# Six slots in the tile of wd for staged weight slices, and squares of wd placed between the last splits of gate and up

## The chip, the cores and the metric

The kernel runs on one core of a Trainium2 chip. The metric is the device time of one execution in microseconds, the median of several runs. The engines are TensorE (PE in the profile; its weight loads PEld), VectorE (DVE), ScalarE (ACT), GpSimd (POOL) and SyncE (SP), which does nothing here but issue DMA transfers, one after another in the order of the program.

## The reference

One transformer block whose two layer norms are modulated by a condition c: multi-query attention with 32 heads of width 16 over 2048 positions, then a feed-forward part with a bilinear gate, F = 1792.

```python
mod = (_silu(c) @ w_mod).reshape(c.shape[0], 6, 1, -1)
sa, ca, ga, sb, cb, gb = (mod[:, 0], mod[:, 1], mod[:, 2], mod[:, 3], mod[:, 4], mod[:, 5])
h = _layernorm(x, axis=-1) * (1 + ca) + sa
x = x + ga * _A_ref(h, A_wq, A_wk, A_wv, A_wo)          # softmax(q k^T / 4) v @ wo, one k and v for all heads
h = _layernorm(x, axis=-1) * (1 + cb) + sb
x = x + gb * _B_ref(h, B_w_gate, B_w_up, B_w_down)      # ((h @ w_gate) * (h @ w_up)) @ w_down
```

Everything is float32. The kernel reaches that precision by splitting each operand of a large product into two float16 halves, a high one and the rest, and adding three products.

## The kernel before, in words

**The long loop.** Attention is worked off in 32 units (8 blocks of 256 positions by 4 groups of heads), a unit in 16 turns over the keys, a turn in two steps: step = 32 × unit + 2 × turn. In a turn PE makes four score tiles (`sc`, L651), of which ACT takes the exponential (`P<-sc`, L653); four more tiles for the running maximum of the next unit (`mx`, L596), which DVE reduces (L600); the products with v (`pv`, L662); and as many side products (`side`, L506: projections of q, later wo, gate, up and down) as fit between. The order of all this is written out by hand, and every engine works in that order.

**A unit's end.** When a unit's last pv is done, in the second turn of the next unit, `pv_out` copies the result (`ev`, ACT L668) and issues ten transfers in a row on SP: two of row sums (`rs`, L673) and eight of 16 rows each (`oc`, L679). `normalise` then loads the row sums (`rc`, L686), takes reciprocals on DVE (L689) and spreads them (`ri`, `rr`). `load_q` fetches the q of the next unit (`sst<-qd`, L561), and `max_rows` writes the finished maxima to the same tile (`sst<-mt`, L634); both are SP transfers that PE's next scores or maxima need.

**The late weights.** `late_weights` makes a list of items for wo, gate, up and down (wd) that need their scales first. `side_step` takes at most one item per step, when the gap of the one before it is over; an item with `nothing` in the middle leaves its function for the start of the next turn. The list has these parts:

- `norms`: each of 36 slices (4 of wo, 16 of gate, 16 of up) is staged by an SP transfer (`stage`, L923, tile `wsl`, three buffers under the tag "xl"); an item later POOL squares it and adds it to an accumulator (`square`, L930 and L932). The accumulators `ssqs` and, from before, the blocks `hfs` of the first layer norm are both views of one large tile, kwb, whose place later holds the halves of wd. `ssqs[0]` serves wo and then gate, `ssqs[1]` up. Three items after a matrix is through, `sums` adds the partitions up on PE (L942), four matmuls a sum, four sums a matrix.
- `gcols`, `tr`, `bc`, `scales`, `inverse`: scales from the sums.
- `pipelined` for wo, gate and up: each slice is staged again, and an item later POOL scales it and writes its two halves (`split`, L1058 or L1064, L1065, L1066).
- `row_norms` for wd: each of 14 slices is staged, and two items later ACT squares it with a sum along the row (L976).
- `last_column` to `last_inverse`: the scale of wd.
- at the second unit, `dlist` is appended: the splits of wd, 14 slices with gap 2.25.

**kwb's layout.** In units of one slot of 512 float32 per partition, `hfs` is slots 0 to 11; `ssqs[0]` begins at slot 4 and is 3.5 slots long, `ssqs[1]` begins at slot 8:

```python
hfs = kwb[:, 0:2 * NHF * BT].bitcast(F32).rearrange("p (n t) -> p n t", n=NHF)
ssqs = [kwb[:, 2 * n * BT:2 * n * BT + 2 * F].bitcast(F32) for n in (KC, 2 * KC)]
```

The program tracks which parts of a tile an instruction reads and writes, and adds waits where they overlap. A transfer also waits for the eighth transfer before it: there are eight lanes, DMAHW0 to DMAHW7, taken in turn.

Of the kernel before, what the change touches and what calls it, by code (L numbers as in the profile page):

```python
# [13 lines left out]
F32 = mybir.dt.float32  # L14
F16 = mybir.dt.float16
AF = mybir.ActivationFunctionType
# [3 lines left out]
S, D, H, DH, F = 2048, 512, 32, 16, 1792  # L20
KC = D // 128
# [8 lines left out]
LEAD = 30  # L30
WARM = (21, 3, 2, 3)
SQ_GAP = 2.75
ROW_GAP = 1.75
SUM_GAP = 6.0
SUM_LAG = 3
SPLIT_GAPS = (2.25, 2.25)
LATE_Q = 3
NORM_AT = (5, 12, 18)
NBANK = 8
# [21 lines left out]
def adaln_mqa_glu_kernel(ctx: ExitStack, tc: tile.TileContext, x_in, wq_in, wk_in, wv_in, wo_in,  # L61
                         wg_in, wu_in, wd_in, c_in, wm_in, out):
    nc = tc.nc
# [5 lines left out]
    work = ctx.enter_context(tc.tile_pool(name="work", bufs=2))  # L69
# [7 lines left out]
    def ps_hold(name="side", shape=(128, 512)):  # L77

        tag, bufs = pool.popleft()
        t = psum.tile(list(shape), F32, name=name, tag=tag, bufs=bufs)  # L80
        held[id(t)] = (t, tag, bufs)
        return t
# [60 lines left out]
    for i in range(3):  # L143
        t = consts.tile([128, 2, BT], F16, name=f"sst{i}")
# [77 lines left out]
    hfs = kwb[:, 0:2 * NHF * BT].bitcast(F32).rearrange("p (n t) -> p n t", n=NHF)  # L222
# [595 lines left out]
    W = {}  # L818
# [56 lines left out]
    def wslices():  # L875
        for k in range(KC):
            yield 3, (k, slice(0, D)), wo_in[k * 128:(k + 1) * 128, :], D
        for m, v in ((0, wgv), (1, wuv)):
            for k in range(KC):
                for c in range(F // GC):  # L880
                    yield m, (k, slice(c * GC, (c + 1) * GC)), v[:, k, c * GC:(c + 1) * GC], GC
        for f in range(FT):
            yield 2, (f, slice(0, D)), wdv[:, f, :], D

    def late_weights():
        st = {}

        def m0(k):
            def f():
                if k == 0:  # L890
                    st["p"] = ps_hold("misc")
                for j, (w, col) in enumerate(((wmB[0], 0), (wmB[0], 512), (wmA, 1024), (wmB[0], 1024))):
                    nc.tensor.matmul(st["p"][32 * j:32 * j + 32, :], silr[:, k, 0:32], w[:, k, col:col + 512],
                                     start=(k == 0), stop=(k == KC - 1))
            return f
# [20 lines left out]
        items = []  # L916
        sl = list(wslices())
        gm = work.tile([128, 4], F32, name="gm", bufs=1)
        rown = consts.tile([128, FT], F32, name="rown")

        def stage(n):
            t = work.tile([128, D], F32, name="wsl", tag="xl", bufs=3)
            nc.sync.dma_start(t[:, :sl[n][3]], sl[n][2])  # L923
            st[n] = t

# [8 lines left out]
        def sums(m, j):  # L934
            w = (D if m > 1 else GC) // 4

            def f():
                p = ps_hold("mx")
                st["p"] = p
                for r in range(4):  # L940
                    c = (0 if m > 1 else r * GC) + j * w
                    nc.tensor.matmul(p[32 * r:32 * r + 32, :w], onec, ssqs[m % 3 != 0][:, c:c + w], start=True, stop=True)  # L942

            def g():
                nc.vector.tensor_reduce(cmq[:, m, j:j + 1], st["p"][:, :w], axis=AX.X, op=OP.max)
                ps_give(st["p"])
            return f, g

        def norms(order):
            ns = [n for m in order for n in range(len(sl)) if sl[n][0] == m]  # L950
            out = []
            waiting = deque()
            for j in range(len(ns) + 1):
                def f(j=j):
                    if j < len(ns):
                        stage(ns[j])
                    if j:
                        square(ns[j - 1])
                out.append((SQ_GAP, nothing, f))
                if waiting and j >= waiting[0][0]:  # L960
                    out.append((0,) + sums(*waiting.popleft()[1:]))
                m = sl[ns[j - 1]][0] if j else None
                if m is not None and (j == len(ns) or sl[ns[j]][0] != m):
                    waiting.extend((j + SUM_LAG, m, n) for n in range(4))
            out.append((SUM_GAP, nothing, nothing))
            return out + [(2,) + sums(*w[1:]) for w in waiting]

        def row_norms(ns):
            out = []
            for j in range(len(ns) + 2):  # L970
                def f(j=j):
                    if j < len(ns):
                        stage(ns[j])
                    if j > 1:
                        t = st[ns[j - 2]]
                        nc.scalar.activation(t, t, AF.Square, accum_out=rown[:, j - 2:j - 1])  # L976
                out.append((ROW_GAP, nothing, f))
            return out

        def gcols():  # L980
# [64 lines left out]
        def split(n):  # L1045
            m, (i, c), v, w = sl[n]

            def load():
                if m < 2 and "g" not in W:
                    W["g"] = big.tile([128, 2, KC, F], F16, name="wg", tag="wg")  # L1050
                    W["u"] = big.tile([128, 2, KC, F], F16, name="wu", tag="wu")
                elif m == 2 and i == 0:
                    W["d"] = big.tile([128, 2, FT, D], F16, name="wd", tag="wd")
                stage(n)

            def gate():
                if m >= 2:
                    nc.gpsimd.tensor_tensor(st[n], st[n], gbb if m == 2 else gab, op=OP.mult)  # L1058

            def halves():  # L1060
                t = st[n][:, :w]
                wt = wo if m == 3 else W["gud"[m]]
                if m < 2:
                    nc.gpsimd.tensor_scalar(t, t, sca[:, m:m + 1], 0.0, op0=OP.mult, op1=OP.add)  # L1064
                nc.gpsimd.tensor_scalar(wt[:, 0, i, c], t, 1.0, 0.0, op0=OP.mult, op1=OP.add)  # L1065
                nc.gpsimd.tensor_tensor(wt[:, 1, i, c], t, wt[:, 0, i, c], op=OP.subtract)  # L1066
            return load, gate, halves

        def pipelined(ns, gap):
            sp = [split(n) for n in ns]  # L1070
            out = []
            for n in range(len(ns) + 1):
                def f(n=n):
                    if n < len(ns):
                        sp[n][0]()
                    if n:
                        sp[n - 1][1]()
                        sp[n - 1][2]()
                out.append((gap, nothing, f))
            return out  # L1080

        n2 = KC + 2 * KC * (F // GC)
        by_column = sorted(range(KC, n2), key=lambda n: sl[n][1][1].start)
        items += pipelined(list(range(KC)) + by_column[:16], SPLIT_GAPS[0]) + pipelined(by_column[16:], SPLIT_GAPS[1])
        items += row_norms(range(n2, len(sl))) + [(1, nothing, last_column), (2, tr, trp), (3, bc, last_scale), (1, nothing, last_inverse)]
        return items, pipelined(list(range(n2, len(sl))), SPLIT_GAPS[0]), [m0(k) for k in range(KC)] + [m1, m2, m3]

    def run_items(items):
        for _, f, post in items:
# [3 lines left out]


    wlist, dlist, mod_rows = late_weights()
    NSTEP = 32
    later = {}
# [258 lines left out]
```

## Time and profile before

| what | us |
|---|---|
| median of 3 runs | 1679.23 (1678.03 to 1679.63) |
| the profiled execution | 1678.16 |
| its span in the profile | 1676.3 |
| PE busy | 1646.6 |
| DVE busy | 1402.8 |
| ACT busy | 1236.5 |
| POOL busy | 523.7 |
| mean granted clock of PE | 0.995 |

The page gives for each group of instructions the line, the engine, the operation, the tiles, the count, the busy time and the mean, and behind the second bar the idle time that the engine had just before them and what ended it. The groups that fill a turn are these, out of section 5 of the page:

```profile
L600 DVE TENSOR_REDUCE mpart<-mx 128x1 f32<-128x512 f32 x2016 | 1274.6, 684 | 110.2 <-PE mx L596 89.4
L653 ACT ACTIVATE P<-sc 128x512 f32<-128x512 f32 x2048 | 1096.0, 599 | 273.6 <-PE sc L651 224.3
L651 PE MATMUL sc<-sst,kst 50*128 50x512 f16 (+1 forms) x2294 | 695.4, 356 | 2.9 <-DMA sst<-mt 2.7
L662 PE MATMUL pv<-P,vst 128*32 128x512 f32 x4096 | 547.1, 606 | 0.9
```

The span in 40 slices shows that POOL and the DMA engines are loaded in the first third alone, where the late weights are staged and split (a digit is a tenth of a slice of 41.9 us):

```profile
POOL 5766638891481011301122011310122101210322
...
DMA  6213213333120000000000000000000000000000
```

### The profile page before, as it was taken

The page shows a single profiled execution, that of the slowest core. Times are in us where ns is not written, and L with a number is a line of the kernel's source. Part 1 is how long each engine was busy: PE and PEld are TensorE (multiplying, and loading weights), DVE is VectorE, ACT ScalarE, POOL GpSimd, SP SyncE. Part 2 cuts the span into 40 slices and gives each one's busy share as a digit, 9 for nine tenths or more (in the row PEclk, how much of TensorE's full clock was granted, in tenths as well). Part 3 has the DMA queues.
Part 4 walks back from the last instruction along what each step waited for, and adds up shares of the span by engine and source line. Part 5 has one row for each costly group of instructions (what it writes and reads, how often), then busy time and mean ns, then how long its engine had stood idle before and what let it go on. Part 6 is the DMA issues. An engine that isn't in the chain of part 4 may idle for free.

```text
span 1676.3 us, 39873 instructions
## 1 busy us (share of the span) xinstructions
PE 1646.6 (98%) x15603; PEld 747.5 (45%) x15603; DVE 1402.8 (84%) x2434; ACT 1236.5 (74%) x2389; POOL 523.7 (31%) x833
## 2 busy tenths in 40 slices
PE   8899999998999999999999999999999999999999
PEld 4333333254533455434544354543545334553776
DVE  7999999897988999999998999999998999880311
ACT  5688888877868777777878777777778777877200
POOL 5766638891481011301122011310122101210322
PEclk9999999999999999999999999999999999999999
DMA  6213213333120000000000000000000000000000
GB/s 239 97 57 94 86 48 108 89 92 94 53 66 19 17 13 26 13 19 20 14 24 8 19 17 25 14 13 19 20 26 6 13 22 26 13 9 14 27 13 13
DMA packets 66024, 67.27 MB, mean 40 GB/s; under 512 B 21542, under 2 KB 50730, under 8 KB 65836
## 3 DMA queue, kind: packets, MB, share of 16 engines
q1 hardware_dynamic: 63724, 64.15, 12.4%
q8 instruction: 122, 2.00, 0.5%
q10 hardware_dynamic: 2112, 0.59, 0.1%
q14 instruction: 66, 0.54, 0.1%
HBM read 51.32 MB, written 8.92 MB: 36 GB/s over the span
## 4 chain that ended last, share of the span: by engine, by line
PE 89%; ACT 3%; DVE 3%; POOL 2%; DMA 2%; SPq 1%; issue 1%; ACTq 0%; POOLq 0%; DVEq 0%
PE side L506 40%; PE pv L662 29%; PE sc L651 10%; PE mx L596 8%; ACT P L653 2%; DVE mpart L600 2%; SPq L679 1%; POOL wsl L1058 1%; DMA xbig<-in_A_x_dram 1%; POOL wd L1066 1%; PE mx L797 1%; ACT hf L805 0%; PE mxt L624 0%; PE sc L596 0%; DMA wsl<-in_B_w_down_dram 0%
## 5 line engine op out<-in xcount | busy, mean ns | idle before, releaser
L600 DVE TENSOR_REDUCE mpart<-mx 128x1 f32<-128x512 f32 x2016 | 1274.6, 684 | 110.2 <-PE mx L596 89.4
L653 ACT ACTIVATE P<-sc 128x512 f32<-128x512 f32 x2048 | 1096.0, 599 | 273.6 <-PE sc L651 224.3
L651 PE MATMUL sc<-sst,kst 50*128 50x512 f16 (+1 forms) x2294 | 695.4, 356 | 2.9 <-DMA sst<-mt 2.7
L596 PE MATMUL mx<-kst,sst 48*128 48x512 f16 x2032 | 636.5, 378 | 11.6 <-ACT P L653 7.0
L662 PE MATMUL pv<-P,vst 128*32 128x512 f32 x4096 | 547.1, 606 | 0.9
L506 PE MATMUL side<-h2T,wg 64*128 64x256 f16 (+1 forms) x2368 | 533.3, 271 | 0.8 <-ACT P L653 0.2
L506 PE MATMUL side<-h2T,wu 64*128 64x256 f16 (+1 forms) x2368 | 531.2, 270 | 0.0
L506 PEld LDWEIGHTS <-wg 64*128 64x128 f16 (+1 forms) x2368 | 223.5, 95 | 223.7 <-ACT P L653 189.6
L506 PE MATMUL side<-wd,glu 64*128 64x512 f16 (+1 forms) x1164 | 266.5, 378 | 0.4 <-ACT P L653 0.4
L651 PEld LDWEIGHTS <-kst 50*128 50x128 f16 x2294 | 209.3, 94 | 85.6 <-issue 65.5
L506 PEld LDWEIGHTS <-wu 64*128 64x128 f16 (+1 forms) x2368 | 223.5, 95 | 48.5 <-issue 12.5
L842 POOL TENSOR_SCALAR glu<-gf 128x256 f16<-128x256 f32 x112 | 45.7, 408 | 630.7 <-DVE gf L841 590.8
L596 PEld LDWEIGHTS <-sst 48*128 48x128 f16 x2064 | 191.2, 94 | 35.8 <-issue 13.0
L506 PEld LDWEIGHTS <-glu 64*128 64x128 f16 (+1 forms) x1164 | 97.2, 95 | 194.1 <-ACT P L653 90.2
L662 PEld LDWEIGHTS pv<-P,vst 128*32 128x32 f32 x4096 | 80.9, 108 | 162.1 <-issue 151.1
L841 DVE TENSOR_TENSOR gf<-side,g 128x256 f32<-128x256 f32 x112 | 46.7, 418 | 77.1 <-ACT g L839 65.2
L506 PE MATMUL side<-h,wq 64*128 64x512 f16 (+1 forms) x372 | 95.9, 376 | 0.5 <-ACT P L653 0.4
L839 ACT ACTIVATE g<-side 128x256 f32<-128x256 f32 x112 | 42.4, 379 | 73.0 <-PE side L506 72.7
L698 POOL TENSOR_TENSOR oc<-oc,rr 128x256 f32<-128x256 f32 x31 | 22.6, 728 | 224.7 <-DMA sst<-qd 132.8
L506 PE MATMUL side<-wo,och 64*128 64x512 f16 (+1 forms) x360 | 86.9, 380 | 0.0
L843 POOL TENSOR_TENSOR glu<-gf,glu 128x256 f16<-128x256 f32 x112 | 75.3, 673 | 9.3
L506 PEld LDWEIGHTS <-och 64*128 64x128 f16 (+1 forms) x360 | 30.7, 94 | 66.9 <-ACT P L653 29.3
(232 smaller groups left out, 789.3 us busy)
## 6 DMA issues: line engine op xcount, KB each, us to landing
wsl<-in_B_w_gate_dram SPq DMA_DIRECT2D x32, 224.0 KB
wsl<-in_B_w_up_dram SPq DMA_DIRECT2D x32, 224.0 KB
wsl<-in_B_w_down_dram SPq DMA_DIRECT2D x28, 256.0 KB
sst<-qd SPq DMA_DIRECT2D x180, 32.0 KB
qd<-q SPq DMA_DIRECT2D x16, 256.0 KB
oc<-ev SPq DMA_DIRECT2D x256, 16.0 KB
rr<-ri SPq DMA_DIRECT2D x32, 128.0 KB
x<-in_A_x_dram SPq DMA_DIRECT2D x14, 256.0 KB
```

What stands on the lines that cost most here:

```text
L506: return nc.tensor.matmul(self.p[:, c * w:(c + 1) * w], left[rows], right[rows], start=start and c == 0, stop=stop and c == len(terms) - 1)
L596: nc.tensor.matmul(m, s[64 * a:64 * a + 48, p, t * 128:(t + 1) * 128], w[64 * a:64 * a + 48, :], start=(i == 0), stop=(i == len(keys) - 1))
L600: nc.vector.tensor_reduce(part, m, axis=AX.X, op=OP.max)
L651: nc.tensor.matmul(t[:, c0:c1], kst[64 * a:64 * a + 50, kt * 128:(kt + 1) * 128], s[64 * a:64 * a + 50, p, c0:c1], start=True, stop=True)
L653: ex = nc.scalar.activation(ptl[u, kt, p, a], t, AF.Exp)
L662: nc.tensor.matmul(pvb[u][32 * j:32 * j + 32, :], vst[:, kt, :], ptl[u, kt, p, a], start=(kt == 0), stop=(kt == KT - 1))
L679: nc.sync.dma_start(oc[u][r:r + 16, :], ev[32 * j:32 * j + 16, c * ST:(c + 1) * ST])
L698: eng.tensor_tensor(o, o, st["r"], op=OP.mult)
L839: nc.scalar.activation(g, p[:, 0:ST], AF.Copy, scale=2.0 ** -45)
L841: nc.vector.tensor_tensor(gf, p[:, ST:2 * ST], g, op=OP.mult)
L842: nc.gpsimd.tensor_scalar(glu()[:, 0, f, :], gf, 1.0, 0.0, op0=OP.mult, op1=OP.add)
L843: nc.gpsimd.tensor_tensor(glu()[:, 1, f, :], gf, glu()[:, 0, f, :], op=OP.subtract)
```

## The change

Four things are changed, all in `late_weights` and its constants:

1. `stage` puts a slice into one of six slots of `hfs`, slots 0, 1, 2, 3, 6 and 7 in turn, as long as the tile of wd is not yet allotted; after that, for the splits of wd, into the three buffers under "xl" as before.
2. The row items of wd, with a lag of 4 items rather than 2 between staging and square, are put after each of the last 15 items of the splits of gate and up; the last four follow by themselves.
3. The gap of the splits goes from 2.25 to 2.5 steps for wo, gate and up (with a row item between two of them they come every 3 steps), and to 3 for wd. Splits begin at step 136 (137 before), row items run from step 194 to 239 (222 to 249), splits of wd from 246 to 288 (257 to 289).
4. The pause ahead of up's sums goes from 6 to 5.

```diff
-ROW_GAP = 1.75
-SUM_GAP = 6.0
+ROW_LAG = 4
+SLOTS = (0, 1, 2, 3, 6, 7)
+SUM_GAP = 5.0
 SUM_LAG = 3
-SPLIT_GAPS = (2.25, 2.25)
+SPLIT_GAP = 2.5
+LAST_GAP = 3.0
...
+        taken = [0]
+
         def stage(n):
-            t = work.tile([128, D], F32, name="wsl", tag="xl", bufs=3)
+            if "d" in W:
+                t = work.tile([128, D], F32, name="wsl", tag="xl", bufs=3)
+            else:
+                t = hfs[:, SLOTS[taken[0] % len(SLOTS)], :]
+                taken[0] += 1
             nc.sync.dma_start(t[:, :sl[n][3]], sl[n][2])
             st[n] = t
...
-            for j in range(len(ns) + 2):
+            for j in range(len(ns) + ROW_LAG):
                 def f(j=j):
                     if j < len(ns):
                         stage(ns[j])
-                    if j > 1:
-                        t = st[ns[j - 2]]
-                        nc.scalar.activation(t, t, AF.Square, accum_out=rown[:, j - 2:j - 1])
-                out.append((ROW_GAP, nothing, f))
+                    if j >= ROW_LAG:
+                        t, n = st[ns[j - ROW_LAG]], j - ROW_LAG
+                        nc.scalar.activation(t, t, AF.Square, accum_out=rown[:, n:n + 1])
+                out.append((0, nothing, f))
...
-        items += pipelined(list(range(KC)) + by_column[:16], SPLIT_GAPS[0]) + pipelined(by_column[16:], SPLIT_GAPS[1])
-        items += row_norms(range(n2, len(sl))) + [(1, nothing, last_column), (2, tr, trp), (3, bc, last_scale), (1, nothing, last_inverse)]
-        return items, pipelined(list(range(n2, len(sl))), SPLIT_GAPS[0]), [m0(k) for k in range(KC)] + [m1, m2, m3]
+        rows_of = row_norms(range(n2, len(sl)))
+        for n, item in enumerate(pipelined(list(range(KC)) + by_column)):
+            items.append(item)
+            if n >= KC + 18 and rows_of:
+                items.append(rows_of.pop(0))
+        items += [(1, nothing, f) for _, _, f in rows_of] + [(1, nothing, last_column), (2, tr, trp), (3, bc, last_scale), (1, nothing, last_inverse)]
+        return items, pipelined(list(range(n2, len(sl))), LAST_GAP), [m0(k) for k in range(KC)] + [m1, m2, m3]
```

After the change the lines stand some places lower: `stage` is L931, `square` L938 and L940, the sums L950, the squares of wd L984, the splits L1066 and L1072 to L1074.

How the change moves instructions is seen in three places. The first is PE at the first sum of gate. Its four matmuls read ssqs[0] (a part of kwb_181) into a tile mx; a wait on DMAHW1 is one for a transfer of that lane, one on Pool for an instruction of POOL. Before:

```order
L662 MATMUL pv_2454<-P_2487,vst_126 32x512
L942 MATMUL mx_2546<-kwb_181,onec_135 32x112 [waits Activation_49,Pool_49]
L942 MATMUL mx_2546<-kwb_181,onec_135 32x112 [waits Pool_49] x3
L651 LDWEIGHTS kst_132
L651 MATMUL sc_2553<-sst2_130,kst_132 128x512 [waits DVE_49]
L596 LDWEIGHTS sst0_128
```

And now:

```order
L664 MATMUL pv_2432<-P_2464,vst_126 32x512
L950 MATMUL mx_2522<-kwb_181,onec_135 32x112 [waits Activation_49,Pool_49]
L950 MATMUL mx_2522<-kwb_181,onec_135 32x112 [waits Pool_49] x2
L950 MATMUL mx_2522<-kwb_181,onec_135 32x112 [waits DMAHW1_49,Pool_49]
L653 LDWEIGHTS kst_132
L653 MATMUL sc_2529<-sst2_130,kst_132 128x512 [waits DVE_49]
```

The matmuls stand where they did; the fourth, which reads columns 1344 to 1455 of the accumulator (slot 6), now waits for a transfer too. That transfer is the third slice of up, on SP, at the same time:

```order
L681 DMA oc_2420<-ev_2418 16x256 [waits DMAHW5_49]
L681 DMA oc_2420<-ev_2418 16x256 [waits DMAHW6_49]
L681 DMA oc_2420<-ev_2418 16x256 [waits DMAHW7_49]
L681 DMA oc_2420<-ev_2418 16x256 [waits DMAHW0_49]
L931 DMA kwb_181<-in_B_w_up_dram 128x448 [waits DMAHW1_49,Pool_49]
L688 DMA rc_2475<-rs1_2421 128x16 [waits DMAHW2_49]
L931 DMA kwb_181<-in_B_w_up_dram 128x448 [waits DMAHW3_49]
```

It stands behind the last of the eight `oc` transfers of unit 1, as it did before; only its target has become a slot of kwb.

The third place is ACT at the ninth square of wd, in unit 7. Now:

```order
L655 ACTIVATE P_6254<-sc_6255 128x512 [waits PE_49,Activation_49]
L841 ACTIVATE g_6260<-side_6053 128x256 [waits DVE_49]
L984 ACTIVATE kwb_181,rown_417<-kwb_181 128x512 [waits DMAHW1_49]
L655 ACTIVATE P_6277<-sc_6278 128x512 [waits PE_49,Activation_49]
L655 ACTIVATE P_6288<-sc_6289 128x512 [waits PE_49,Activation_49]
```

The lane is that of the twelfth slice of wd, which takes the slot of the ninth, and on SP stands so:

```order
L681 DMA oc_6139<-ev_6137 16x256 [waits DMAHW6_49]
L681 DMA oc_6139<-ev_6137 16x256 [waits DMAHW7_49]
L681 DMA oc_6139<-ev_6137 16x256 [waits DMAHW0_49]
L931 DMA kwb_181<-in_B_w_down_dram 128x512 [waits DMAHW1_49]
L688 DMA rc_6207<-rs6_6140 128x16 [waits DMAHW2_49]
```

Before, the third slice of wd stood in this place of the queue, and the third square waited for it.

More of the change, by code (lines that the diff above doesn't have):

```diff
@@ L1067, in split, with pipelined @@
             return load, gate, halves
-        def pipelined(ns, gap):
+        def pipelined(ns, gap=SPLIT_GAP):
             sp = [split(n) for n in ns]
```

## The prediction

> **What bounds the kernel now.** I read the engines' shares and the chain of waits first, on the page of the profile:
>
> ```profile
> PE 1646.6 (98%) x15603; PEld 747.5 (45%) x15603; DVE 1402.8 (84%) x2434; ACT 1236.5 (74%) x2389; POOL 523.7 (31%) x833
> ...
> PE 89%; ACT 3%; DVE 3%; POOL 2%; DMA 2%; SPq 1%; issue 1%; ACTq 0%; POOLq 0%; DVEq 0%
> ```
>
> TensorE (PE) is busy for 98% of the span and carries 89% of the chain. The change takes no matmul away, so it can only give back the time in which PE stands still or runs at half clock. What PE waits for, between 60 and 600 us (the stretch in which late_weights works), stands in the view of waits (total us, times, longest):
>
> ```profile
> PE mx L596 <- ACT P L653: 7.0, 2, 6.8
> PE sc L651 <- DMA sst<-mt: 2.7, 1, 2.7
> PE mx L596 <- DMA sst<-qd: 2.6, 1, 2.6
> ```
>
> Three stops, 12.3 us together, are all that is large. The clock comes on top. The table of stretches (busy time of PE, PEld, DVE, ACT, POOL, then the granted clock, DMA share and GB/s) shows where PE ran at half speed:
>
> ```profile
> 160.00:200.00 40.00, 40.00 (x345) 13.76 (x345) 39.63 (x70) 34.31 (x67) 20.55 (x24) 1.00 0.30 90
> 318.00:322.00 4.00, 2.23 (x20) 0.61 (x22) 1.52 (x3) 1.17 (x3) 3.75 (x5) 1.00 0.50 156
> 390.40:397.20 6.80, 4.31 (x26) 1.70 (x27) 1.72 (x4) 4.03 (x10) 1.07 (x2) 0.50 0.48 149
> 482.60:486.00 3.40, 3.40 (x17) 0.60 (x15) 2.10 (x4) 1.53 (x3) 3.14 (x5) 0.50 0.27 78
> ```
>
> The 6.8 us stop was followed by 6.8 us at 0.50, the 2.7 us stop by 3.4 us at 0.50, the 2.6 us stop (its window is the second row) by none. Time at 0.50 costs half of the PE work done in it: 4.31/2 = 2.2 us and 3.40/2 = 1.7 us. The first row is a stretch without stops: PE 40.00 of 40 and DVE 39.63 of 40. Nothing there can be made up later.
>
> **The change part by part.** Costs are against the profiled execution, 1678.16 us (span 1676.3); the median of the runs, 1679.23, lies 1.07 above it.
>
> *Sums of gate: a new wait.* Slots 6 and 7 lie inside ssqs[0], the accumulator of gate's squares. Its sums on PE read columns 1344 and up, and slots 6 and 7 are by then the targets of w_up's third and fourth slices. So the fourth matmul of the first sum now waits for a DMA (lane DMAHW1), which stands on SyncE (SP) behind pv_out's burst of two rs and eight oc transfers. In the trace of before that place reads, on SP, POOL and PE:
>
> ```profile
> 164.16 5.01 SPq L679 DMA_DIRECT2D oc<-ev  x8
> 169.28 0.52 SPq L923 DMA_DIRECT2D wsl<-in_B_w_up_dram  x1
> ...
> 170.37 0.86 SPq L923 DMA_DIRECT2D wsl<-in_B_w_up_dram  x2
> ...
> 172.09 0.93 POOL L930 TENSOR_TENSOR kwb<-wsl 128x448 f32<-128x448 f32 x1 [11.45 <-DMA wsl<-in_B_w_up_dram]
> ...
> 167.38 0.38 PE L942 MATMUL mx<-kwb,onec 128*32 128x112 f32 x8
> ```
>
> The slice is issued at 169.28 and POOL, idle, takes it up at 172.09; the sum starts at 167.38. Before, PE didn't care. Now it stands 172.1 − 167.4 = 4.7 us, and all that is queued behind the matmul stands with it: scores, maxima, pv, and so ACT's exps and DVE's reduces. The slice can't come earlier through the added slots, since what holds it is ev, and not a buffer (the order of SP around it is unchanged). A stop of 2.7 us brought one half-clock window of 3.4 us, so I add 1.7: **+6.4 us**. Bounds: +4.7 without the clock, +8.1 with two windows. The second sum waits for the fourth slice, issued 1.1 us later but needed only at the next sum, one turn on: nothing.
>
> The Trainium skill ("TensorE: Matmul & The Clock Gate", Part 1) says that the clock falls after an idle window of about 3.4 us that runs free. By it the 4.7 us stop may or may not hold a whole idle window, and the term would be 4.7 or 6.4. The trace is stricter than the page: a stop of 2.68 us was enough here.
>
> *Squares of wd: shorter cover.* Before, a run of row items stood alone after the splits; the third slice lay behind the burst of the next unit, and ACT waited for it with the exps queued behind:
>
> ```profile
> 381.36 0.68 ACT L668 ACTIVATE ev<-pv,evs 128x512 f32<-128x512 f32 x1
> ...
> 384.45 0.67 ACT L976 ACTIVATE wsl<-wsl 128x512 f32<-128x512 f32 x1
> ...
> 391.64 0.63 ACT L976 ACTIVATE wsl<-wsl 128x512 f32<-128x512 f32 x1 [6.43 <-DMA wsl<-in_B_w_down_dram]
> ...
> 383.22 5.32 SPq L679 DMA_DIRECT2D oc<-ev  x8
> 388.64 0.52 SPq L923 DMA_DIRECT2D wsl<-in_B_w_down_dram  x1
> ...
> 392.89 0.58 PE L596 MATMUL mx<-kst,sst 48*128 48x512 f16 x1 [6.81 <-ACT P L653]
> ...
> 464.27 2.25 ACT L653 ACTIVATE P<-sc 128x512 f32<-128x512 f32 x4 [0.65 <-PE sc L651]
> ...
> 470.02 2.19 ACT L653 ACTIVATE P<-sc 128x512 f32<-128x512 f32 x4 [0.65 <-PE sc L651]
> ```
>
> The last two rows are undisturbed turns, two of them in 5.75 us: 2.87 us each. The stop cost 6.8 + 2.2 = 9.0 us. The new lag of four items seems to cover any burst. It doesn't: with rows and splits in turn, six slots hold three rows, so slice n+3 lands in the slot of slice n before the square of n (item n+4) reads it. Each square waits for a DMA issued one row item, 3 steps, earlier. The ninth (step 230, a turn's start) waits for the twelfth slice, and that one stands on SP right behind the burst of the same unit 7, whose ev is at 381.36. The square comes one turn later than the stalled one did: in before's times 385.2 + 2.9 = 388.1 against a landing at 391.6. ACT still waits 3.5 us, PE some 3.9, and a stop of 3.9 brings a half-clock window: 3.9 + 1.7 = 5.6. **−3.4 us**. Bounds: −9.0 (the burst comes early enough) to +0 (the square stands as early as before). The other squares have 3 steps of cover, and a step is half a turn of 2.87 us, so 4.3 us, against 391.64 − 388.64 = 3.0 from issue to landing. 1.3 us is left; I take nothing for them, and +2 for the range.
>
> *Slots six deep.* Before, SP stood in the staging of w_up (a slot not yet freed by POOL) while the queue's next transfers, the q rows of load_q, were wanted:
>
> ```profile
> 309.24 6.64 SPq L923 DMA_DIRECT2D wsl<-in_B_w_up_dram  x3
> 315.96 3.17 SPq L561 DMA_DIRECT2D sst<-qd  x6
> ...
> 319.77 0.39 PE L596 MATMUL mx<-kst,sst 48*128 48x512 f16 x1 [2.56 <-DMA sst<-qd]
> ```
>
> With six slots the slot was freed three splits earlier and SP walks through. The stop goes: −2.56, of which I count **−2.3** (ACT's exps would have held part of that turn). Bounds −2.6 and 0. The same blocking put rc late, where DVE waited:
>
> ```profile
> 348.64 0.25 DVE L689 RECIPROCAL rc<-rc 128x16 f32<-128x16 f32 x1 [1.12 <-DMA rc<-rs]
> ```
>
> **−0.6**, between 0 and −1.1.
>
> *Splits of wd three steps apart.* In 447 to 496 POOL is the queue that is late:
>
> ```profile
> 447.00:496.00 49.00, 46.22 (x457) 20.56 (x453) 41.66 (x71) 35.18 (x68) 45.23 (x51) 0.97 0.29 89
> ...
> L1058 POOL TENSOR_TENSOR wsl<-wsl,gbb 128x512 f32<-128x512 f32 x14 | 17.8, 1271 | 2.0 <-DMA wsl<-in_B_w_down_dram 2.0
> L1066 POOL TENSOR_TENSOR wd<-wsl,wd 128x512 f16<-128x512 f32 x14 | 16.2, 1156 | 1.2
> L1065 POOL TENSOR_SCALAR wd<-wsl 128x512 f16<-128x512 f32 x14 | 8.6, 618 | 1.2
> L843 POOL TENSOR_TENSOR glu<-gf,glu 128x256 f16<-128x256 f32 x5 | 3.4, 672 | 0.4
> ...
> 465.38 13.65 SPq L923 DMA_DIRECT2D wsl<-in_B_w_down_dram  x4
> 479.12 1.19 SPq L634 DMA_DIRECT2D sst<-mt  x2
> ...
> 481.48 0.39 PE L651 MATMUL sc<-sst,kst 50*128 50x512 f16 x1 [2.68 <-DMA sst<-mt]
> ```
>
> A split takes 1.27 + 0.62 + 1.16 + some 0.13 of gaps = 3.18 us. At 2.25 steps of 1.44 us a split comes every 3.23 us: POOL 98% full with splits alone, and glu's halves on top put it behind. SP stood 13.65 us in four stagings and issued the running maxima (sst<-mt) at 479.12, too late. At 3 steps a split comes every 4.3 us, 74% of POOL; the five pairs of glu (1.1 us each) and one normalise (1.8) add 7.3/49 = 15%. No backlog, SP issues the maxima on time: 2.7 + 1.7 = **−4.4 us**. Bounds: −4.7 and 0. The last split starts at step 288, as before (289), so the down projection sees wd when it did. Twelve steps were won ahead of it; they pay for the slower pace.
>
> *The rest.* Up's sums keep their step. Gate's and up's splits come every 3 steps at the end rather than 2.25; a split of 448 columns is shorter than wd's and POOL isn't full there. The last four squares fall two to a turn, 2.19 + 2 × 0.63 us of ACT in a turn of 2.87, 0.6 over in each of two turns; that before's squares, one in nearly every turn from 392 on, are spread thinner gives about as much back: 0 together.
>
> Sum: +6.4 − 3.4 − 2.3 − 0.6 − 4.4 = **−4.3**. 1678.2 − 4.3 = 1673.9, and with the 1.07 of the median **1675.0 us**.
>
> **The rivals.**
> 1. *The gate sum doesn't stop PE.* If the slice lands before PE reaches the sum, only gains are left: −10.7, 1668.5. For it: only the order of eight small transfers puts the slice there. Against it: ev, the burst and POOL's own 11.45 us wait are all in the trace, and nothing ahead of 164 moves. Chance 0.10.
> 2. *The burst clears the squares.* If ACT's ninth square comes late enough, the whole 9.0 goes: 1669.4. For it: any delay of ACT in unit 7 adds to the cover, 3.5 us would do. Against it: pv_out's ev is delayed by the same. Chance 0.13.
> 3. *Slower: the squares wait one by one.* Place: ACT, turns 104 to 117. A row slice stands on SP behind a w_up slice that waits for POOL (its slot is freed by the split three before). If SP lags by more than the 1.3 us of slack, ten squares wait with the exps behind them; at a lag of 2.5 us each costs 1.2, 12 us in all, less what ACT's idle time (0.65 in a turn) takes, 10 × 0.65: +5.5, and with the ninth at its old 9.0 another +3.4. 1675.0 + 8.9 = 1684. It decides from a lag of 2 us on. For it: SP stood 6.64 us in three stagings at 309 in just this way. Against it: twice the slots, and POOL has air at 3 steps. Chance 0.20.
> 4. *Nothing is won.* The ninth square keeps its full 9.0 (the bound +0), the sum takes two half-clock windows (8.1): 1675.0 + 3.4 + 1.7 = 1680. Chance 0.12.
>
> The forecast has the remaining 0.45, and with its own terms' bounds lies in 1671 to 1678.
>
> **How the numbers follow.** This kernel's runs differ by 0.1%; about 0.2%, 3.4 us, is what can be told from no change. Faster therefore means under 1675.9. Rivals 1 and 2 are there (0.23); of the forecast, which sits 0.9 us inside the border, 0.27. Rivals 3 and 4 give slower 0.20 + 0.03, and 2 to 5 us may have escaped me on either side: faster 0.50, same 0.26, slower 0.24. The range must reach rivals 1 and 2 at its foot and most of 3 at its head: 1667 to 1683.
>
> **What would show it.** In the profile after, right: a new group in the waits of PE at the sums of gate (L950, releaser DMA, wsl's successor kwb<-in_B_w_up) of 4 to 5 us near 167 to 172 and a slice with a clock of 0.5 behind it; no stop at sst<-qd near 317 and none at sst<-mt near 480; one stop of ACT at the squares (L984) in unit 7, 3 to 4 us, on a w_down DMA. Wrong: PE going through 167 without a stop (rival 1), no DMA among the releasers of L984 (rival 2), many of them (rival 3), or SP still standing in the staging of wd ahead of sst<-mt, which would say that POOL's pace was not the cause.

## The result and the profile after

| | before | after |
|---|---|---|
| median of 12 runs, us | 1678.33 (1677.19 to 1679.63) | 1676.86 (1673.67 to 1678.76) |
| profiled execution, us | 1678.16 | 1676.62 |
| its span, us | 1676.3 | 1674.8 |

The ratio is 0.9990, with a 95% interval from 0.9981 to 0.9999: 1.5 us less, at the edge of what can be told from nothing. The predicted 1675.0 lies 1.9 us below the measured 1676.86, and the range of 1667 to 1683 holds it. The outcome that was given the best chance, faster by more than 0.2%, did not come.

A small difference can be the sum of large ones. The program is regular, so the first exponential of each unit cuts the two traces at the same places. The table gives the length, from one such start to the next, of the units in which the two kernels differ by more than 0.4 us. All others agree within 0.3 us; units 12 on add 0.3 in all.

```
unit            2      5      6      7      8      9
before      41.21  48.57  44.60  56.39  49.16  50.21
after       48.44  45.98  46.45  52.82  46.24  48.60
difference  +7.23  -2.59  +1.85  -3.57  -2.92  -1.61      sum -1.61
forecast    +6.4   -2.3   -0.6   -3.4   -4.4 (8 and 9)    sum -4.3
```

Units 2, 5, 7 and 8 with 9 came as the prediction had them. Unit 6 did not: a gain of 0.6 was written down and a loss of 1.9 came.

The view of PE's waits of the changed kernel, 60 to 600 us (total us, times, longest):

```profile
PE mx L598 <- ACT P L655: 5.7, 3, 3.3
PE mx L950 <- DMA kwb<-in_B_w_up_dram: 4.4, 1, 4.4
```

The two stops at transfers to sst are gone, in their place stands one at the sums (L950), and the wait for ACT is in three pieces, the largest 3.3 rather than 6.8. A piece of 2.2 us in unit 6 is new; the 3.3 are what was left in unit 7.

### The profile page after: what moved, and what is told of

Same layout as the page of the kernel before. It is cut to its first block, busy times and chain, and to the rows that moved or that the text cites. A ratio compares the mean times of both kernels' runs of the same rounds, so it can differ in the third digit from the quotient of the medians.

```text
span 1674.8 us, 39843 instructions
## 1 busy us (share of the span) xinstructions
PE 1647.2 (98%) x15603; PEld 745.8 (45%) x15603; DVE 1403.3 (84%) x2434; ACT 1236.2 (74%) x2389; POOL 525.3 (31%) x833
## 4 chain that ended last, share of the span: by engine, by line
PE 90%; ACT 3%; DVE 3%; DMA 2%; SPq 1%; issue 1%; POOL 0%; ACTq 0%; DVEq 0%
PE side L508 40%; PE pv L664 29%; PE sc L653 10%; PE mx L598 8%; ACT P L655 2%; DVE mpart L602 1%; SPq L681 1%; DMA xbig<-in_A_x_dram 1%; PE mx L799 1%; DMA kwb<-in_B_w_up_dram 0%; ACT hf L807 0%; DMA kwb<-in_B_w_down_dram 0%; PE mxt L626 0%; PE sc L598 0%; DVE bs L247 0%
```

## Unit 2: the sum behind a slice of up

From the timeline of the changed kernel (start, duration, and in brackets the idle time before it): SP, POOL, PE.

```profile
164.12 5.01 SPq L681 DMA_DIRECT2D oc<-ev  x8
169.24 0.52 SPq L931 DMA_DIRECT2D kwb<-in_B_w_up_dram  x1
...
172.13 0.93 POOL L938 TENSOR_TENSOR kwb<-kwb 128x448 f32<-128x448 f32 x1 [11.00 <-DMA kwb<-in_B_w_up_dram]
...
172.13 0.55 PE L950 MATMUL mx<-kwb,onec 128*32 128x112 f32 x2 [4.42 <-DMA kwb<-in_B_w_up_dram]
```

PE takes its fourth matmul up in the same hundredth of a microsecond as POOL takes the slice: 172.13. The stop is 4.4 us where 4.7 were forecast. The rest is clock. Here are three windows of the changed kernel (busy PE, PEld, DVE, ACT, POOL, then the granted clock):

```profile
167.50:170.90 3.40, 0.21 (x10) 0.00 (x0) 0.40 (x1) 0.52 (x1) 0.00 (x0) 1.00 0.15 32
171.00:174.30 3.30, 2.17 (x11) 0.77 (x12) 1.15 (x3) 0.98 (x2) 2.08 (x3) 0.50 0.63 192
174.40:177.70 3.30, 3.30 (x18) 0.53 (x16) 1.70 (x3) 1.20 (x3) 3.22 (x4) 0.50 0.00 0
```

Two windows at 0.50 and not the one that was counted: (2.17 + 3.30)/2 = 2.7 us, and 4.4 + 2.7 = 7.1 of the measured 7.23.

The test gives the norms slots 0 to 3 alone, which lie ahead of the accumulator:

```diff
-                t = hfs[:, SLOTS[taken[0] % len(SLOTS)], :]
+                slots = SLOTS if "g" in W or "o" in st else SLOTS[:4]
+                t = hfs[:, slots[taken[0] % len(slots)], :]
...
             def load():
...
+                st["o"] = True
                 stage(n)
```

> While the norms run, slices go to slots 0 to 3 alone, which share nothing with gate's accumulator; splits and row items use the six slots as in the changed kernel. Theory (the fourth matmul of gate's first sum stood 4.4 us for the third slice of up, and two turns after it lost 2.8 more to the half clock): no wait of L950's line on a transfer, turns of 2.5 and 2.7 us there, 7.2 us less than the changed kernel: 1669.6. Rival (four slots are too few, and POOL's squares or the sums then wait elsewhere; or the stop moves to the next sum): a stop of 2 us or more stays between 160 and 235 us, 1673 or above.

Measured: 1669.75 us (1669.50 to 1671.99), 0.9954 of the kernel before with an interval of 0.9939 to 0.9969. Unit 2 is back at 41.22 us. All eight matmuls of the first two sums of gate are in one piece:

```profile
167.22 0.38 PE L951 MATMUL mx<-kwb,onec 128*32 128x112 f32 x8
```

Four slots are enough for the norms. The loss in unit 2 came from where two of the six slots lie.

## Units 6 and 7: squares that wait for a younger slice

The ninth square did what the prediction said, down to the burst ahead of its slice. ACT and SP of the changed kernel:

```profile
397.69 0.63 ACT L984 ACTIVATE kwb<-kwb 128x512 f32<-128x512 f32 x1 [3.56 <-DMA kwb<-in_B_w_down_dram]
...
389.69 5.13 SPq L681 DMA_DIRECT2D oc<-ev  x8
394.87 0.58 SPq L931 DMA_DIRECT2D kwb<-in_B_w_down_dram  x1
```

3.56 us where 3.5 were forecast. In unit 6 there is a second wait of that kind, for which the prediction had 1.3 us of slack and no cost:

```profile
362.18 0.63 ACT L984 ACTIVATE kwb<-kwb 128x512 f32<-128x512 f32 x1 [2.64 <-DMA kwb<-in_B_w_down_dram]
...
350.83 0.42 SPq L931 DMA_DIRECT2D kwb<-in_B_w_down_dram  x1
352.32 0.33 SPq L693 DMA_DIRECT2D ri<-rc  x1
357.05 0.67 SPq L695 DMA_DIRECT2D rr<-ri  x1
...
358.27 0.42 SPq L931 DMA_DIRECT2D kwb<-in_B_w_down_dram  x1
...
359.22 0.42 SPq L931 DMA_DIRECT2D kwb<-in_B_w_down_dram  x1
```

The slice that the square waits for is the second of the two behind `rr`, issued at 359.22 and landed at 362.18: 3.0 us, as assumed. What was not assumed is how late it was issued. SP stood between `ri` and `rr`, and the view of SP's waits from 330 to 375 us says on what, for the kernel before and for the changed one:

```profile
SPq L693 <- DMA ri<-rc: 1.4, 1, 1.4
```

```profile
SPq L695 <- DMA ri<-rc: 4.3, 1, 4.3
```

`rr` reads in DRAM what `ri` writes there, so it waits for `ri` to land. Just ahead of `ri` SP has now issued five slices of 224 or 256 KB within 2.4 us, three of them rows of wd. SP stood 4.3 us for the 8 KB of `ri` to land instead of 1.4, and the two row slices behind `rr` came that much later. 1.3 us of slack were less than the 2.9 us added; ahead of `ri` SP had stood another 1.0 us for the reciprocals.

That `ri` is what made the slice late is read from this trace; no run keeps the shared slots and takes away the wait for `ri` alone. The size varies between traces of the same code: with slots 0 to 3 for the norms unit 6 took 46.32 us, in the run with splits of wd at 2.25 steps (below) 45.48, against 46.45 here.

To see whether the two waits are the whole loss, the row slices get slots of their own, so that the square of slice n, four row items after its transfer, no longer finds slice n+3 in its slot:

```diff
+ROWS = (4, 5, 8, 9, 10, 11)
...
-        def stage(n):
+        def stage(n, row=None):
...
+            elif row is not None:
+                t = hfs[:, ROWS[row % len(ROWS)], :]
...
-                        stage(ns[j])
+                        stage(ns[j], j)
```

> The row slices of wd get six slots of their own (4, 5, 8 to 11), so that a square, four row items after its transfer, no longer finds a younger slice in its slot. All else as in the changed kernel, the sum's stop included. Theory (the squares waited for a slice staged one row item before, 2.64 and 3.56 us, and this took 2.5 us in unit 6 and 4 to 6 in unit 7): no idle time of ACT before the squares by a transfer of wd, 6.5 to 8 us less than the changed kernel: 1669 to 1670.4. Rival (the loss in unit 7 is ACT's own load, with two squares in some turns, and the burst delays something else): only the 2.5 of unit 6 and part of the rest go, 1673 to 1674.5.

Measured: 1669.44 us (1668.60 to 1670.56), 0.9950 of before with an interval of 0.9935 to 0.9964. No square waits for a transfer in this trace; unit 6 takes 43.74 and unit 7 47.66 us. Against the changed kernel that is 2.7 and 5.2 us less. The 5.2 are the residue for which the prediction had 5.6. SP still waited 4.1 us for `ri` in this run: nothing hung on it any more.

Both edits in one kernel:

> Both edits together: slots 0 to 3 while the norms run, and slots of their own for the row slices. Theory: the two losses lie 190 us apart and add, 14 to 15 us less than the changed kernel: 1662 to 1663. Rival: one hides part of the other, or a new wait comes up once they are gone: 1665 to 1668.

Measured: 1662.15 us (1661.34 to 1663.12), 0.9905 with an interval of 0.9888 to 0.9921. The two losses add: 7.1 and 7.4 us alone, 14.7 together. This is 15.7 us faster than the kernel before in the same session. Without the two losses the change would have been worth that much; with them it kept 1.5.

## Units 5, 8 and 9: which part of the change gave the gains

The prediction put the gain of units 8 and 9 down to POOL's pace and that of unit 5 to the depth of the staging. In both cases the change does two things at once. The first test puts the splits of wd back to 2.25 steps in the changed kernel:

```diff
-LAST_GAP = 3.0
+LAST_GAP = 2.25
```

> The changed kernel with the splits of wd 2.25 steps apart, as before, and all else unchanged. Theory (POOL's pace, 98% full with splits alone, put SP and the running maxima behind): the stop at sst<-mt comes back at some unit's end, +4.4 with its half-clock window: about 1681. Rival (it was gone because the splits of wd start 11 steps earlier and end before the maxima are due): no change, 1676.9.

Measured: 1677.04 us (1674.34 to 1678.19), no change against 1676.86. The rival holds. SP's waits between 460 and 482 us before, and between 460 and 480 us in this run:

```profile
SPq L923 <- POOL wd L1066: 15.8, 5, 4.7
```

```profile
SPq L931 <- POOL wd L1074: 6.2, 2, 3.4
SPq L636 <- ACT mt L631: 5.0, 1, 5.0
```

At the old pace SP does wait for POOL, but only 6.2 us, and then it is early: it stands 5.0 us for the maxima (`mt`) to be written. The splits began 11 steps earlier, and 9.3 of the 15.5 us that SP waited for POOL between 425 and 498 us were over by 460.

The changed kernel itself, at 3 steps, waits longer for POOL between 460 and 480 us than this run does. Its waits, and then SP ahead of the maxima, first in the changed kernel and then in this run:

```profile
SPq L931 <- POOL wd L1074: 11.3, 4, 4.7
SPq L636 <- ACT mt L631: 1.7, 1, 1.7
...
465.50 8.73 SPq L931 DMA_DIRECT2D wsl<-in_B_w_down_dram  x3
476.05 1.19 SPq L636 DMA_DIRECT2D sst<-mt  x2
```

```profile
470.53 0.37 SPq L931 DMA_DIRECT2D wsl<-in_B_w_down_dram  x1
475.97 1.18 SPq L636 DMA_DIRECT2D sst<-mt  x2
```

The prediction had named SP standing in the staging of wd ahead of `sst<-mt` as a sign that POOL's pace was not the cause. The sign came: the backlog is still there, only with three stagings ahead of the maxima where the kernel before had four, so that SP is through 1.7 us before the maxima are written. So is the pace worth nothing? The reverse test slows the splits of wd in the kernel before:

```diff
-        return items, pipelined(list(range(n2, len(sl))), SPLIT_GAPS[0]), [m0(k) for k in range(KC)] + [m1, m2, m3]
+        return items, pipelined(list(range(n2, len(sl))), 3.0), [m0(k) for k in range(KC)] + [m1, m2, m3]
```

> The kernel before with the splits of wd 3 steps apart and nothing else changed; they start at step 257 as before and end at 299 rather than 289. Theory (pace: POOL at 98% with splits 2.25 steps apart puts SP and the running maxima behind): the stop of 2.68 us at sst<-mt near 480 goes with its half-clock window, 4.4 to 4.6 us less than before: about 1673.3. Rival (only the earlier start of the splits keeps SP free ahead of the maxima; slower splits from the same start meet the maxima too): the stop stays at 1 us or more, or the down projection, which starts near 496, waits for the last slices: within 1 us of before, or slower.

Measured: 1673.54 us (1673.09 to 1676.05), 0.9973 of before with an interval of 0.9963 to 0.9984. Units 8 and 9 together take 94.73 us instead of 99.37. SP in that run:

```profile
458.62 9.78 SPq L923 DMA_DIRECT2D wsl<-in_B_w_down_dram  x3
472.79 1.20 SPq L634 DMA_DIRECT2D sst<-mt  x2
```

It waits for POOL here too, but again in three stagings instead of four. So either part suffices: a slower pace from the same start, or an earlier start at the same pace, the latter tried only with the other parts of the change in place. Both put fewer stagings between `load_q` and the maxima. The down projection waited for neither. By itself this one number is worth more than the whole change.

For unit 5, the kernel with own slots for the rows, with three slots in place of six for all else (0 to 2, which also takes gate's accumulator out of the way):

```diff
-SLOTS = (0, 1, 2, 3, 6, 7)
+SLOTS = (0, 1, 2)
```

> As the run with own slots for the row slices, but all other slices go to three slots, 0 to 2, in place of six; none of them touches gate's accumulator. So against the run of both edits (1662.15) only the depth is taken away. Theory (the stop of 2.56 us at sst<-qd near 317 and the late rc went because six slots let SP run ahead): they come back, +2.5 to +3.5: about 1665. Rival (they went because splits are 2.5 steps apart and POOL keeps up): no stop there, within 1 us of 1662.2.

Measured: 1662.26 us (1661.43 to 1663.01). No stop at sst<-qd; unit 5 takes 45.98 us, as with six. The rival holds again: depth is not needed to remove the stop. SP in this run:

```profile
304.70 0.41 SPq L934 DMA_DIRECT2D kwb<-in_B_w_gate_dram  x1
305.54 0.33 SPq L934 DMA_DIRECT2D kwb<-in_B_w_up_dram  x1
305.96 2.72 SPq L564 DMA_DIRECT2D sst<-qd  x6
310.55 4.57 SPq L934 DMA_DIRECT2D kwb<-in_B_w_up_dram  x2
```

Between the burst and load_q stand six stagings where the kernel before had eight, and SP waits 4.2 us for POOL from 296 us on until load_q rather than 14.1. It waits behind load_q instead, where nothing hangs on it. Then six slots at the old pace:

```diff
-SPLIT_GAP = 2.5
+SPLIT_GAP = 2.25
```

> The run of both edits (1662.15) with the splits of wo, gate and up 2.25 steps apart as in the kernel before, six slots kept; row items still go between the last splits. With the run on three slots it tells whether depth removes the stop at sst<-qd near 317 by itself. Theory (either suffices: with six slots SP never waits for POOL there, whatever the pace): no stop at sst<-qd, no reciprocal waiting for rc, within 1 us of 1662.2. Rival (pace alone did it): a stop of 1.5 to 2.6 us near 317 comes back in spite of six slots, 1664 to 1665.

Measured: 1662.91 us (1662.58 to 1663.19), unit 5 at 45.98 us, no stop. SP in that run, where it stood 6.64 us in the staging before:

```profile
305.84 1.35 SPq L935 DMA_DIRECT2D kwb<-in_B_w_up_dram  x3
307.29 2.72 SPq L564 DMA_DIRECT2D sst<-qd  x6
```

Three stagings take 1.35 us, and load_q follows 8.7 us earlier than before (315.96). Again either part is enough: a slower pace puts fewer stagings ahead of load_q, and free slots let SP pass them almost without waiting. Both runs also have the splits begin one step earlier than before; what that step gives by itself, with three slots at the old pace, no run shows. The stop is also not of a fixed size: in the run with the slower wd in the kernel before, in which nothing ahead of it was changed, it was 1.93 us instead of 2.56.

## What is left of the row work

In the run with both edits some turns of unit 7 are still longer than the usual 2.9 us: 3.59, 3.13 and 3.28. To see what the squares cost at all, they and their transfers were left out; the sums of rows are a constant in this run:

```diff
+        nc.gpsimd.memset(rown, 1.0)
...
-                        stage(ns[j], j)
+                        pass
...
-                        t, n = st[ns[j - ROW_LAG]], j - ROW_LAG
-                        nc.scalar.activation(t, t, AF.Square, accum_out=rown[:, n:n + 1])
+                        pass
```

> The run of both edits with the row work of wd left out: no slice of wd is staged for its squares and none is squared; the sums of rows are a constant. Theory (with own slots the squares cost only ACT's time where two fall into a turn, turns of 3.59, 3.13 and 3.28 us in unit 7 instead of 2.9): 1.5 us less than that run: 1660.6. Rival (ACT's 14 squares of 0.83 us cost in every turn that has one, or the transfers cost elsewhere): 4 us less or more: 1658.

Measured: 1660.61 us (1659.68 to 1660.84), 1.5 less than with both edits, as expected. In the trace only 0.96 are in unit 7 (46.69 against 47.65), and the turn of 3.28 is there without squares too. What else is shorter lies in pieces of at most 0.3 us in units 8 and on, which hold no squares, and ahead of unit 0. With no row slices around, SP's wait for `ri` fell to 2.7 us:

```profile
SPq L696 <- DMA ri<-rc: 2.7, 1, 2.7
```

It was 4.0 to 4.6 in every run that stages row slices between the splits, with three slots or six, at either pace. So row slices make up 1.3 to 1.9 us of it, whatever the depth. Why 2.7 are left where the kernel before had 1.4 stays open.

The last run keeps the row work, with one square a turn at the end:

```diff
-        items += [(1, nothing, f) for _, _, f in rows_of] + ...
+        items += [(2, nothing, f) for _, _, f in rows_of] + ...
...
-LAST_GAP = 3.0
+LAST_GAP = 2.75
```

> The run of both edits with the last four row items 2 steps apart rather than 1 (a square a turn), and the splits of wd 2.75 steps apart so that they still end in time. Theory: the turns of 3.59, 3.13 and 3.28 us in unit 7 fall to about 3, 1 us less: 1661.1. Rival (the same ACT time is only moved, or POOL falls behind at 2.75): 1662.2 or above.

Measured: 1661.17 us (1661.02 to 1662.15), 0.9900 with an interval of 0.9884 to 0.9917. Unit 7 is 0.3 us shorter than with both edits: the turn of 3.59 stays, the next falls from 3.13 to 2.65. That is less than the 1 us that was expected, and the medians' difference of 1.0 lies within the runs' own spread: of the 1.9 us between the two profiled executions 1.5 lie ahead of the first unit (see the last section). Among the kernels that do all of the work this is the fastest, by a hair.

## Why the prediction was right, and where it was not

The range held, but it is 16 us wide and holds the time of the kernel before as well. What bears the prediction out is the table of units. The time came 1.9 us off and not 2.7, as the sum did, by luck: the 1.07 us added for the median came from three runs, and over twelve the median lies 0.2 above the profiled execution.

- **The sum of gate (+6.4).** Right in place, cause and sign; measured +7.23. The stop was 4.4 for 4.7, and the clock cost 2.7 for 1.7. The term that was mis-sized is "one half-clock window": there were two, which the bound of +8.1 allowed for. Shown by the run with slots 0 to 3. By the order of the program the sharing is more than a wait: slices were staged over columns of gate's accumulator while it was being filled, so that parts of its sums are made of raw weights. Only a scale hangs on them; no run here shows what that does to the precision.
- **The ninth square (−3.4).** Right; unit 7 gave −3.57, and the residue of 5.6 measured 5.2.
- **The other squares (nothing, +2 for the range).** Wrong. This is the step that failed: "1.3 us is left; I take nothing for them". The mechanism was in the third rival, but its place was looked for in the wrong wait. It named a row slice behind a slice of up that waits for POOL. What came was a row slice behind `rr`, which waits for `ri`, which lies behind the row slices themselves. One square waited instead of ten (a second by 0.3 us), 2.64 us, and cost 2.7. The estimate of slack used the landing time of the slice alone and not what SP waits for ahead of it in the queue.
- **load_q (−2.3).** Unit 5 gave −2.59, the whole stop. The reason given, six slots, is one of two that each suffice in the runs tried.
- **rc (−0.6).** DVE no longer waits for rc, but unit 6 as a whole lost: the gain, if there was one, lies under the 2.7. In the run with own row slots unit 6 takes 43.74 us against 44.60 before, 0.9 less, of which this was a part at most.
- **The splits of wd (−4.4).** −4.5 in units 8 and 9, right in size. The reason failed: "No backlog" did not come true, as SP still stood 8.73 us in three stagings at 465.50. The slower pace does remove the stop, by putting fewer stagings ahead of the maxima. And the sentence that the twelve steps won "pay for the slower pace" had it the wrong way round: the earlier start alone would have done.
- **The rest (0).** The turns with two squares were there, 3.59 and 3.13 us; the run without row work puts all squares at 1.0 us in the trace once nothing waits.

The sum was off by 2.7 us, and its two large errors have one sign: +0.8 in unit 2, from the second half-clock window, and +2.45 in unit 6, less 0.6 elsewhere.

## What to carry to other kernels

Before a buffer is laid into a tile that something else still uses, list who reads which columns until when: here two of six slots cost 7 us by where they lay. In a ring that two streams share, a lag counted in items of one stream is half as long as it looks. A queue that runs ahead does not only arrive early; it can also put its bulk ahead of small transfers on whose landing the same queue then stands. And when a change bundles a slower pace with an earlier start or a deeper ring, undo them one at a time: here each half was enough, and one number in the old kernel gave 4.9 us. Then look at the wait that was to go: SP's wait for POOL stayed while the stop behind it went.

## What the runs showed of the hardware

The half clock after a stop is not a fixed price. After the stops shown here it came in pieces of 3.4 us (one window) or 6.8 (two). A stop of 2.56 us (before, at 317) and one of 2.20 us (changed kernel, at 361) brought none, the 2.68 us before brought one window, the 3.27 us in unit 7 of the changed kernel brought one, and the 4.42 us two. Nearly the same stop in unit 7 brought two with 3.51 us in the run with splits of wd at 2.25 steps, and one with 3.77 us in the run with slots 0 to 3. Here are windows of the changed kernel, then of the run with splits of wd at 2.25 steps:

```profile
396.20:399.60 3.40, 0.65 (x10) 0.42 (x13) 0.72 (x2) 1.91 (x5) 0.00 (x0) 1.00 0.79 232
399.70:403.00 3.30, 3.30 (x22) 1.27 (x16) 1.04 (x2) 2.07 (x6) 3.05 (x5) 0.50 0.33 125
403.10:406.50 3.40, 3.40 (x45) 2.00 (x40) 2.79 (x6) 2.45 (x6) 1.22 (x2) 1.00 0.02 5
```

```profile
393.00:396.30 3.30, 1.66 (x23) 1.16 (x20) 2.61 (x5) 0.11 (x1) 1.07 (x2) 1.00 0.39 92
396.40:399.70 3.30, 1.54 (x10) 0.62 (x13) 0.69 (x1) 2.61 (x6) 1.07 (x2) 0.50 0.84 286
399.80:403.10 3.30, 3.30 (x25) 1.51 (x19) 0.69 (x1) 1.84 (x6) 3.05 (x5) 0.50 0.01 5
```

In the first the stop lies in one window of 3.4 us, and in the next PE is busy throughout. In the second it straddles a border: the window with 1.66 us of work is followed by half clock, the one with 1.54 by half clock again, and the clock came back one window later. So where a stop falls between the borders seems to decide whether it costs some 1.7 us more. That is read from these traces and was not tried by itself. PE's busy time in a window is not the whole measure: in the run without row work 2.34 us of work were followed by half clock, and in the kernel before, at the stop of 2.56 us, 1.89 us were not (the row behind it, 318 to 322, is in the prediction, with 1.00). The rows of the run without row work come first:

```profile
39.11:42.52 3.41, 2.34 (x20) 1.08 (x12) 3.41 (x6) 3.38 (x8) 3.16 (x5) 1.00 0.94 360
42.53:45.90 3.37, 3.07 (x8) 1.93 (x9) 3.37 (x6) 2.46 (x8) 3.20 (x4) 0.50 1.02 425
```

```profile
315.32:318.73 3.41, 1.89 (x16) 0.34 (x9) 2.58 (x5) 2.98 (x6) 3.16 (x6) 1.00 0.47 104
```

The clock also spreads the runs. The runs of the kernels with stops lie 2.4 us (before) and 5.1 us (changed) apart, 12 runs each; those of the two kernels with row slots of their own and a free accumulator 1.8 and 1.6, with 4 runs each. The profiled executions of these two are 1662.89 us (both edits) and 1661.43 us (three slots), and the whole difference lies ahead of the first unit, whose first exponential starts at 77.44 and 75.97. The first had a half-clock window there that the second had not; the row with 0.50 is of the run with both edits:

```profile
19.20:22.50 3.30, 3.30 (x25) 1.20 (x18) 3.06 (x14) 0.80 (x2) 2.62 (x10) 0.50 1.04 390
...
19.20:22.50 3.30, 3.30 (x28) 1.23 (x20) 3.06 (x14) 1.78 (x3) 2.62 (x10) 1.00 1.03 377
```

So differences under 1.5 us between medians of four runs can come from ahead of the first unit; the lengths of the units are free of that. Whether the larger spread of the kernels with stops has the same reason was not tried.
